# The last two blocks' gate, choice and ranking in another order, expert 0's gate weights by themselves, and one looped body for further tiles

## The chip, the core and the metric

The kernel runs on one core of a Trainium2 chip. The core has five engines that work side by side, each through its own instructions in order: TensorE (PE in the profile, with its weight loads as PEld), VectorE (DVE), ScalarE (ACT), GpSimd (POOL) and SyncE (SP, which here only starts DMA transfers). They wait for one another by semaphores. The metric is the device time of one execution in microseconds (us); less is better.

## What is computed

Attention over 4 x 576 tokens with 8 heads, a dense layer with g = h cos(h), and a mixture of 8 experts of which every token uses two. The part that matters here is the third:

```python
def _moe2_ref(x, w_gate, w_noise, noise, w1, w2):          # x: 2304 x 512
    noisy_logits = x @ w_gate + np.log1p(np.exp(x @ w_noise)) * noise
    top2 = np.argpartition(-noisy_logits, 2, axis=1)[:, :2]
    top2_w = softmax of the two chosen logits
    for e in range(8):                                     # w1: 512 x 1024, w2: 1024 x 512
        for k in range(2):
            mask = top2[:, k] == e
            h = np.maximum(x[mask] @ w1[e], 0.0)
            out[mask] += top2_w[mask, k, None] * (h @ w2[e])
```

All of it is float32. The kernel writes each float32 operand as a sum of two fp32r halves ("hi" and "lo") and runs three matmul passes (hi x hi, hi x lo, lo x hi) where float32 accuracy is wanted. Making the two halves is called a split: ACT copies the hi half, another engine subtracts it from the original to give the lo half.

## The kernel before

The 2304 tokens go through attention and the dense layer as 9 blocks of 256 tokens (blocks 0 to 8, `NBLK` = 9, `LAST` = 8). For each block there are 8 pairs p: `g1` gives the hidden values (PE, L562), `post` turns them into g (ACT and DVE, with a last subtraction on POOL, L570 to L579) and `g2` adds them into two output tiles in PSUM (PE `acc`, L589). The pairs are the steps 0 to 71 of one loop, with `g2` two steps behind `g1`; the table `BESIDE` says which other work is put beside which step and at which of four places in it (-1, 0, 1, 2). Scheduling is manual: on every engine the instructions run in the order in which the Python code issues them.

When a block's `acc` tiles are complete, its tokens are sent to the experts in a chain of small steps: `r_rows` (the block's rows x leave PSUM and go to DRAM `x1d`), `r_trans` (PE transposes, tiles `mx`, `x1t`), `r_gate` (PE, `mg`, `lp`), `r_logits` (PE `ml`, DVE `lg`, `az`), `r_exp` (ACT), `r_top`, `r_top2` (DVE, the softplus of the noise as a series, tile `po`), `r_pick` (DVE, the two best experts of each token, ending in the tile `os`), `r_rank` (PE counts the tokens ahead, tile `mr`; DVE makes slots `si` from it) and `r_send` (POOL, four indirect DMAs that write token number and logit difference into the table `tab`). For blocks 0 to 7 these steps lie beside later blocks' matmuls. For block 8 there is no later block; they lie beside the first half of expert 0.

An expert has room for 608 tokens in five tiles (128, 128, 96 and 128, 128). `m_g1(e, half, f)` makes hidden chunk f of 8 for the first 352 tokens (half 0, PE L903 `pe`, input `xga`) or for the other 256 (half 1, input `xgb`); ACT (L905) and DVE (L906) evacuate it as the halves of `h`, through two PSUM buffers `ph` (in half 0 of expert 0 every second f uses the buffers of `acc` instead). `m_y(e, t)` multiplies `h` with the second weight (PE L938 `ye`), `m_out` scales by the gate weight and sends the rows to `out`. Expert 0's first 352 tokens are final before the last two blocks are ranked, so its half 0 starts right after block 8's last `acc` matmul. Its tiles 3 and 4 can only be gathered when block 8's sends have landed: `t_load` reads `tab` back (SP, `tb`), `t_gather` fetches the rows (POOL, `xg`), `t_trans` transposes them (PE `mgx` L886) and splits them into `xgb` (ACT L888, DVE L889). `t_weights` makes all gate weights from `tb` (L852 to L861, with one exp on ACT).

Expert weights are loaded as `wraw` and split by `split_we(e, k, q)` into `we` (ACT L819; L820 on DVE, or on POOL where the call says so); expert 0 has 16 such pieces of 128 x 512.

At the end, DVE reduces the token counts `cnt` (L1094 to L1100), every engine loads one number (L1101), and a branch (L1102) jumps over code for tokens beyond an expert's 608. With these inputs that code is not executed. It stands there eight times, once for each expert, each with a loop of its own.

Of the kernel before, what the change touches and what calls it, by code (L numbers as in the profile page):

```python
# [9 lines left out]
F32 = mybir.dt.float32  # L10
# [8 lines left out]
P = 128  # L19
# [7 lines left out]
DM = 512  # L27
# [172 lines left out]
70:2 r_pick(7)  # L200
71:2 r_rank(7)
# [6 lines left out]
def kernel(ctx: ExitStack, tc: tile.TileContext, qT, kT, v, wm, we, wg, noise, out):  # L208
# [408 lines left out]
    def r_gate(blk):  # L617
# [4 lines left out]
        lp = tpool.tile([P, TB], F32, tag="t4", name=f"lp{blk}")  # L622
# [160 lines left out]
    for blk in range(NBLK - 1):  # L783
# [11 lines left out]
        at_step(i0 + d[0] + d[1], 2, r_rank, blk)  # L795
# [49 lines left out]
    def t_weights():  # L845
        weight_of(wts, tb.rearrange("p e t c -> p (e t) c")[:, :, 1])

    def weight_of(dst, d):
# [116 lines left out]
    for q in range(4):  # L965
# [3 lines left out]
        if q < 2:  # L969
            at_step(69, 2, split_we, 0, 1, q)  # L970
# [40 lines left out]
    tasks = {}  # L1011
# [81 lines left out]
    mxc = small.tile([P, 1], F32, tag="mxc", name="mxc", bufs=1)  # L1093
    nc.vector.tensor_reduce(mxc, cnt, axis=AX.X, op=ALU.max)  # L1094
    nti = small.tile([P, NE + 1], I32, tag="nti", name="nti", bufs=1)
    ntf = small.tile([P, NE], F32, tag="ntf", name="ntf", bufs=1)
    nc.vector.tensor_scalar(ntf, cnt, float(CAP), None, op0=ALU.max)
    nc.vector.tensor_scalar(ntf, ntf, 1.0 / P, (63.5 - CAP) / P + NTILE, op0=ALU.mult, op1=ALU.add)
    nc.vector.tensor_copy(nti[:, :NE], ntf)
# [86 lines left out]
```

## Time and profile before

| | |
|---|---|
| time, median of 3 executions | 1034.81 us (1034.64 to 1035.19) |
| the profiled execution's own time | 1032.98 us |
| its span, first to last instruction | 1031.2 us |
| PE matmul busy | 980.9 us (95% of the span) |
| DVE, ACT, POOL busy | 547.5, 458.7, 368.1 us |
| chain of work that ended last, by engine | PE 72%, DVE 13%, ACT 5%, DMA 4% |

The profile lists every instruction with its start, its duration and, where its engine stood idle before it, who released it. The span is the time that instructions cover; the execution's own time is a little longer. Times in the text are us from the start of the span. [...]

### The profile page before, as it was taken

How to read it: one execution, taken by the hardware profiler on the slowest of the kernel's cores; microseconds unless marked ns; L12 is line 12 of the kernel's file. 1: busy time of each engine (PE TensorE's matmuls, PEld its weight loads, DVE VectorE, ACT ScalarE, POOL GpSimd, SP SyncE). 2: the span in 40 equal slices, each digit the busy share in tenths (PEclk: the TensorE clock that was granted, in tenths of full speed). 3: DMA queues.
4: the chain of work that ended last, by engine and by line, in shares of the span. 5: the costliest groups of instructions: out<-in, count | busy, mean ns of one | idle time of the engine just before them, and what ended most of it. 6: DMA issues, size and time to landing. Idle time of an engine off the chain costs nothing.

```text
span 1031.2 us, 16810 instructions
## 1 busy us (share of the span) xinstructions
PE 980.9 (95%) x6560; PEld 864.8 (84%) x6560; DVE 547.5 (53%) x1134; ACT 458.7 (44%) x908; POOL 368.1 (36%) x477
## 2 busy tenths in 40 slices
PE   8797989999999899999999889999999999999995
PEld 6676778988889788898887689898898979898984
DVE  7799885357754655354464556344453536353221
ACT  6646765555645655455554334233232414142110
POOL 5555553243453341323334432231313232322211
PEclk9998999999999999999999999999999999999998
DMA  9962212223312120000054345453434243441201
GB/s 216 328 220 81 80 55 43 85 72 114 96 52 57 40 55 1 21 1 23 21 192 122 84 134 176 140 168 110 156 126 157 76 154 124 157 149 55 67 26 47
DMA packets 70601, 105.19 MB, mean 102 GB/s; under 512 B 31251, under 2 KB 44819, under 8 KB 70512
## 3 DMA queue, kind: packets, MB, share of 16 engines
q1 hardware_dynamic: 60528, 76.34, 24.3%
q0 software_dynamic: 9984, 27.68, 8.7%
q8 instruction: 54, 0.88, 0.4%
q14 instruction: 35, 0.29, 0.1%
HBM read 85.41 MB, written 19.59 MB: 102 GB/s over the span
## 4 chain that ended last, share of the span: by engine, by line
PE 72%; DVE 13%; ACT 5%; DMA 4%; issue 3%; SPq 1%; POOL 1%; ACTq 0%; DVEq 0%; POOLq 0%
PE pe L903 20%; PE ye L938 20%; PE ph L562 13%; PE acc L589 12%; DVE cut L291 3%; DMA raw<-in_wm 2%; PE sc L430 2%; PE mgx L886 2%; DVE cut L290 1%; DVE cut L292 1%; DVE r L571 1%; PE mo L505 1%; DVE po L654 1%; PE mt L485 1%; DVE r L575 1%
## 5 line engine op out<-in xcount | busy, mean ns | idle before, releaser
L562 PE MATMUL ph<-xhl,wm 128*128 128x256 f32 x1728 | 230.0, 289 | 11.6 <-ACT wm L298 4.3
L562 PEld LDWEIGHTS ph<-xhl,wm 128*128 128x128 f32 x1728 | 219.4, 195 | 19.9 <-ACT wm L298 4.7
L938 PE MATMUL ye<-we,h 128*128 128x512 f32 (+1 forms) x960 | 231.0, 397 | 0.0
L589 PE MATMUL acc<-wm,g 128*128 128x512 f32 x864 | 220.3, 398 | 2.8 <-POOL wm L299 0.9
L938 PEld LDWEIGHTS ye<-we,h 128*128 128x128 f32 (+1 forms) x960 | 173.9, 184 | 43.3
L589 PEld LDWEIGHTS acc<-wm,g 128*128 128x128 f32 x864 | 156.8, 190 | 33.7 <-POOL wm L299 1.2
L579 POOL TENSOR_TENSOR g<-r,g 128x512 fp32r<-128x512 f32 x72 | 95.7, 1329 | 207.5 <-ACT g L578 207.4
L903 PE MATMUL pe<-xga,we 128*128 128x352 f32 x768 | 125.4, 323 | 0.0
L903 PEld LDWEIGHTS pe<-xga,we 128*128 128x128 f32 x768 | 122.7, 188 | 0.5 <-issue 0.4
L951 POOL DMA_INDIRECT out<-old,tir x35 | 35.6, 1017 | 221.9 <-DVE old L949 217.1
L906 DVE SCALAR_TENSOR_TENSOR h<-pe,h 128x256 fp32r<-128x256 f32 (+1 forms) x128 | 60.6, 474 | 97.1 <-ACT h L905 96.2
L905 ACT ACTIVATE h<-pe 128x256 fp32r<-128x256 f32 (+1 forms) x128 | 54.2, 424 | 122.2 <-PE pe L903 122.2
L949 DVE SCALAR_TENSOR_TENSOR old<-ye,wts,old 128x512 f32<-128x512 f32 (+1 forms) x35 | 26.3, 750 | 135.5 <-PE ye L938 135.5
L903 PE MATMUL pe<-xgb,we 128*128 128x256 f32 x768 | 95.9, 286 | 1.8 <-DVE xgb L889 1.3
L903 PEld LDWEIGHTS pe<-xgb,we 128*128 128x128 f32 x768 | 94.7, 195 | 2.5 <-DVE xgb L889 1.5
L571 DVE SCALAR_TENSOR_TENSOR r<-r,ph 128x512 f32<-128x512 int32 x72 | 49.1, 682 | 82.9 <-ACT r L570 82.8
L575 DVE SCALAR_TENSOR_TENSOR r<-r,ph 128x512 f32<-128x512 f32 x72 | 49.4, 686 | 82.2 <-ACT r L574 82.0
L820 DVE TENSOR_TENSOR we<-wraw,we 128x512 fp32r<-128x512 f32 x121 | 82.5, 691 | 3.6 <-ACT we L819 0.9
L819 ACT ACTIVATE we<-wraw 128x512 fp32r<-128x512 f32 x128 | 78.4, 623 | 3.2 <-issue 3.2
L573 ACT ACTIVATE r<-r 128x512 f32<-128x512 f32 x72 | 45.4, 631 | 65.5 <-DVE r L571 65.4
L570 ACT ACTIVATE r<-ph 128x512 int32<-128x512 f32 x72 | 42.6, 592 | 51.1 <-PE ph L562 50.9
L578 ACT ACTIVATE g<-r 128x512 fp32r<-128x512 f32 x72 | 45.4, 631 | 43.8 <-DVE r L575 29.5
(181 smaller groups left out, 1035.3 us busy)
## 6 DMA issues: line engine op xcount, KB each, us to landing
wraw<-in_we SPq DMA_DIRECT2D x64, 512.0 KB, 5.7
raw<-in_wm SPq DMA_DIRECT2D x28, 512.0 KB, 9.8
vts<-in_v SPq DMA_DIRECT2D x13, 384.0 KB, 3.9
x1d<-x SPq DMA_DIRECT2D x9, 512.0 KB, 3.6
out<-zt SPq DMA_DIRECT2D x18, 256.0 KB, 3.9
kts<-in_kT SPq DMA_DIRECT2D x13, 288.0 KB, 3.1
qts<-in_qT SPq DMA_DIRECT2D x26, 144.0 KB, 3.9
piece<-in_wm SPq DMA_DIRECT2D x4, 512.0 KB, 4.0
```

The lines of the kernel that those rows point to most:

```text
L562: nc.tensor.matmul(ph[:, j, :], w[:, a, o:o + P], t[:, x, c, :], start=(c == 0 and n == 0 and (j == 0 or len(cs) == 4)), stop=(c == 3 and ...
L571: nc.vector.scalar_tensor_tensor(r, n, -TWO_PI, ph, op0=ALU.mult, op1=ALU.add)
L573: nc.scalar.activation(r, r, AF.Sin, scale=0.5)
L575: nc.vector.scalar_tensor_tensor(r, r, 0.5, ph, op0=ALU.subtract, op1=ALU.mult)
L579: nc.gpsimd.tensor_tensor(g[:, 1, :], r, g[:, 0, :].bitcast(F32), op=ALU.subtract)
L589: nc.tensor.matmul(ACC[blk][t], g[:, a, j * TB + t * P:j * TB + (t + 1) * P], w[:, x, 1024 + j * DM:1024 + (j + 1) * DM], start=(p == 0 an ...
L819: nc.scalar.activation(t[:, 0, fs], raw, AF.Copy)
L820: eng.tensor_tensor(t[:, 1, fs], raw, t[:, 0, fs].bitcast(F32), op=ALU.subtract)
L903: nc.tensor.matmul(ph[:, :n], w[:, a, o:o + P], x[:, b, c, :], start=(c == 0 and i == 0), stop=(c == 3 and i == 2))
L905: nc.scalar.activation(h[:, 0, f, :], ph[:, :n], AF.Relu)
L906: nc.vector.scalar_tensor_tensor(h[:, 1, f, :], ph[:, :n], 0.0, h[:, 0, f, :].bitcast(F32), op0=ALU.max, op1=ALU.subtract)
L938: nc.tensor.matmul(acc, h[:, a, f, o:o + n], w[:, b, (f % 4) * DM:(f % 4 + 1) * DM], start=(f == 0 and i == 0), stop=(f == 7 and i == 2))
```

## The change

It has four parts.

1. In steps 70 and 71, `split_we(0,1,2)` and `split_we(0,1,3)` are done beside the last two pairs of block 8, and `r_pick(7)` moves from step 70 to the end of step 71, with `split_we(0,2,0)` behind it. `r_rank(7)` moves from step 71 to behind the last `g2` and `r_rows(8)`, and `r_send(7)` with it.
2. `r_rows(8)` moves its second half with DVE instead of ACT, ahead of it ACT executes one dummy exp, and block 8's steps are placed anew among expert 0's `m_g1`: the transposes ahead of chunk 0, the gate behind chunk 0, and so on, with the ranking between chunks 6 and 7. The splits of expert 0 that POOL did (its L820 in this stage) are done by DVE. `lp` of block 8 gets another buffer.
3. `t_weights` makes expert 0's five gate weights first (5 columns) and those of experts 1 to 7 (35 columns) behind `m_out(0, 0..2)`.
4. The code for further tokens stands once, in a loop over tiles with a loop over experts in it. It is still jumped over.

```diff
-70:2 r_pick(7)
-71:2 r_rank(7)
+70:1 split_we(0,1,2)
+71:0 split_we(0,1,3)
+71:2 r_pick(7) split_we(0,2,0)
...
     def r_rows(blk):
         for t in range(2):
-            nc.scalar.activation(x[:, t, :], ACC[blk][t], AF.Copy, scale=-2.0)
+            if blk == NBLK - 1 and t:
+                nc.vector.tensor_scalar(x[:, t, :], ACC[blk][t], -2.0, None, op0=ALU.mult)
+            else:
+                nc.scalar.activation(x[:, t, :], ACC[blk][t], AF.Copy, scale=-2.0)
...
     g2(*steps[-2])
-    for t in range(2):
-        r_send(NBLK - 2, t)
     g2(*steps[-1])
     LAST = NBLK - 1
+    nc.scalar.activation(one, one, AF.Exp)
     r_rows(LAST)
+    r_rank(LAST - 1)
+    for t in range(2):
+        r_send(LAST - 1, t)
...
-    for f, t in ((0, r_trans), (1, r_gate), (2, r_logits), (3, r_exp), (3, r_top), (4, r_top2), (5, r_pick), (7, r_rank)):
-        tasks.setdefault(f, []).append(t)
-    late = [(1, 2), (1, 3)] + [(2, q) for q in range(4)] + [(3, 0), (3, 1)]
-    for f in range(8):
-        m_g1(0, 0, f)
-        split_we(0, *late[f], nc.gpsimd if f < 7 else nc.vector)
-        for t in tasks.get(f, []):
-            t(LAST)
-    for q in range(2, 4):
+    r_trans(LAST)
+    m_g1(0, 0, 0)
+    r_gate(LAST)
+    m_g1(0, 0, 1)
+    split_we(0, 2, 1)
+    r_logits(LAST)
+    r_exp(LAST)
+    split_we(0, 2, 2)
+    r_top(LAST)
+    m_g1(0, 0, 2)
+    r_top2(LAST)
+    m_g1(0, 0, 3)
+    r_pick(LAST)
+    for f in range(4, 7):
+        m_g1(0, 0, f)
+    r_rank(LAST)
+    m_g1(0, 0, 7)
+    split_we(0, 2, 3)
+    for q in range(4):
         split_we(0, 3, q)
...
+    t_weights(0, 1)
     t_load(1, NE)
-    t_weights()
...
     for t in range(3):
         m_out(0, t)
+    t_weights(1, NE)
...
     with tc.If(over > CAP):
-        for e in range(NE):
-            nt = nc.values_load(nti[0:1, e:e + 1], min_val=NTILE, max_val=NTILE + -(-(NT - CAP) // P))
-            with tc.For_i(NTILE, nt, 1) as i:
+        nt = nc.values_load(nti[0:1, 1:2], min_val=NTILE, max_val=NTILE + -(-(NT - CAP) // P))
+        with tc.For_i(NTILE, nt, 1) as i:
+            with tc.For_i(0, NE, 1) as e:
```

The first place is DVE in the last two steps of block 8. `r_7` is the tile of the last pair; `oh`, `os` belong to the pick of block 7 and `rb`, `base` to its rank. Before:

```order
L681 CAST fi_5772<-i_5763 128x4
L684 TENSOR_TENSOR oh_5774<-iota_184,fi_5772 128x16 x2
L687 TENSOR_TENSOR os_5777<-oh_5774 128x16
L571 SCALAR_TENSOR_TENSOR r_7_5804<-r_7_5804,ph_7_5779 128x512
L575 SCALAR_TENSOR_TENSOR r_7_5804<-r_7_5804,ph_7_5779 128x512
L699 TENSOR_TENSOR rb_5831<-mr_5825,base 128x16
L701 TENSOR_TENSOR base<-mr_5825,base 128x8
```

And now (`we_1` are the two weight splits):

```order
L576 SCALAR_TENSOR_TENSOR r_6_5741<-r_6_5741,ph_6_5716 128x512
L828 TENSOR_TENSOR we_1_5708<-wraw_0_5497,we_1_5708 128x512
L572 SCALAR_TENSOR_TENSOR r_7_5789<-r_7_5789,ph_7_5764 128x512
L828 TENSOR_TENSOR we_1_5708<-wraw_0_5497,we_1_5708 128x512
L576 SCALAR_TENSOR_TENSOR r_7_5789<-r_7_5789,ph_7_5764 128x512
L680 MAX m_5812<-po_5692 128x8
L681 MAX_INDEX i_5813<-m_5812,po_5692 128x8
```

The pick of block 7 stood ahead of the last pair's two operations on DVE and now stands behind them; two splits stand among them.

The second place is PE behind block 8's last `acc`, among expert 0's chunks `pe_0_0` to `pe_0_7`. Before:

```order
L903 MATMUL pe_0_0_5885<-xga_5594,we_0_5555 128x352 x12
L613 MATMUL mx_0_5903<-ident,x_8_5872 128x128 x4
L613 MATMUL mx_1_5909<-ident,x_8_5872 128x128 x4
L903 MATMUL pe_0_1_5915<-xga_5594,we_0_5555 128x352 x12
L621 MATMUL mg_5932<-x1t_5902,wgn 32x256 x4
L903 MATMUL pe_0_2_5939<-xga_5594,we_0_5555 128x352 x12
L630 MATMUL ml_5957<-ident,lp_5937 128x128 x2
L903 MATMUL pe_0_3_5964<-xga_5594,we_0_5555 128x352 x12
L903 MATMUL pe_0_4_5997<-xga_5594,we_1_5708 128x352 x12
L903 MATMUL pe_0_5_6019<-xga_5594,we_1_5708 128x352 x12
L903 MATMUL pe_0_6_6053<-xga_5594,we_1_5708 128x352 x12
L903 MATMUL pe_0_7_6071<-xga_5594,we_1_5708 128x352 x12
```

And now:

```order
L617 MATMUL mx_0_5893<-ident,x_8_5857 128x128 x4
L617 MATMUL mx_1_5899<-ident,x_8_5857 128x128 x4
L912 MATMUL pe_0_0_5906<-xga_5594,we_0_5555 128x352 x12
L625 MATMUL mg_5921<-x1t_5892,wgn 32x256 x4
L912 MATMUL pe_0_1_5928<-xga_5594,we_0_5555 128x352 x12
L637 MATMUL ml_5945<-ident,lp_5926 128x128 x2
L912 MATMUL pe_0_2_5970<-xga_5594,we_0_5555 128x352 x12
L912 MATMUL pe_0_3_5990<-xga_5594,we_0_5555 128x352 x12
L912 MATMUL pe_0_4_6022<-xga_5594,we_1_5708 128x352 x12
L912 MATMUL pe_0_5_6037<-xga_5594,we_1_5708 128x352 x12
L912 MATMUL pe_0_6_6052<-xga_5594,we_1_5708 128x352 x12
L700 LDWEIGHTS tri
```

Block 8's transposes, gate and logits stand one chunk earlier, and its rank (`tri` is its first operand) stands ahead of the last chunk instead of behind it.

The third place is DVE where expert 0's second half begins. Before:

```order
L820 TENSOR_TENSOR we_1_6144<-wraw_0_6115,we_1_6144 128x512 x4
L852 SCALAR_TENSOR_TENSOR we__6169<-tb 128x40
L854 TENSOR_SCALAR wts<-we__6169 128x40
L855 RECIPROCAL wts<-wts 128x40
L856 TENSOR_SCALAR wn__6170<-tb 128x40
L858 TENSOR_SCALAR wo__6176<-we__6169 128x40
L859 TENSOR_TENSOR wn__6170<-wn__6170,wo__6176 128x40
L860 TENSOR_TENSOR wn__6170<-wn__6170,we__6169 128x40
L861 TENSOR_TENSOR wts<-wts,wn__6170 128x40
L889 TENSOR_TENSOR xgb_6250<-mgx_3_6251,xgb_6250 128x4x128
L889 TENSOR_TENSOR xgb_6250<-mgx_4_6258,xgb_6250 128x4x128
L946 TENSOR_SCALAR new_6275<-ye_0_6181,wts 128x512
```

And now:

```order
L870 TENSOR_TENSOR wts<-wts,wn__6155 128x5
L898 TENSOR_TENSOR xgb_6251<-mgx_3_6252,xgb_6251 128x4x128
L898 TENSOR_TENSOR xgb_6251<-mgx_4_6259,xgb_6251 128x4x128
L955 TENSOR_SCALAR new_6276<-ye_0_6182,wts 128x512
L955 TENSOR_SCALAR new_6282<-ye_1_6207,wts 128x512
L955 TENSOR_SCALAR new_6288<-ye_2_6232,wts 96x512
L861 SCALAR_TENSOR_TENSOR we__6294<-tb 128x35
L863 TENSOR_SCALAR wts<-we__6294 128x35
```

The eight operations on all 40 weights stood ahead of the splits of `xgb`; now eight on 5 columns stand there, and eight on 35 columns behind the three `new`, ahead of the first evacuation of half 1.

## Rows read from the trace of the kernel before

**Rows 1.** Busy time by stretch: stretch, its length, each engine's busy us, PEclk, DMA.

```profile
545.00:604.00 59.00, 49.78 (x266) 41.83 (x266) 30.74 (x88) 20.16 (x39) 28.50 (x39) 0.94 0.42 112
604.00:1019.00 415.00, 414.91 (x2433) 370.67 (x2431) 175.11 (x294) 123.44 (x256) 111.05 (x176) 1.00 0.37 122
1019.00:1031.20 12.20, 0.00 (x0) 0.00 (x0) 1.25 (x6) 0.00 (x0) 1.00 (x1) 0.61 0.09 28
```

**Rows 2.** PE's waits between 540 and 604: total us, times, longest.

```profile
PE mr L693 <- DVE os L687: 5.0, 2, 3.7
PE mgx L886 <- DMA xg<-x1d,tic: 1.4, 2, 1.1
PE pe L903 <- DVE xgb L889: 1.3, 1, 1.3
```

**Rows 3.** Two short stretches, columns as in rows 1.

```profile
574.50:577.90 3.40, 3.37 (x13) 2.70 (x14) 3.30 (x11) 0.42 (x1) 0.82 (x1) 0.50 0.00 0
...
598.40:601.80 3.40, 3.40 (x18) 3.40 (x17) 2.03 (x4) 0.38 (x1) 2.33 (x5) 0.50 0.54 176
```

**Rows 4.** PE in order of time: start, us, line, operation, count, idle before.

```profile
542.09 2.91 PE L589 MATMUL acc<-wm,g 128*128 128x512 f32 x12
...
551.08 2.56 PE L589 MATMUL acc<-wm,g 128*128 128x512 f32 x10 [0.68 <-POOL spacer L713]
...
561.01 9.78 PE L903 MATMUL pe<-xga,we 128*128 128x352 f32 x60
...
574.68 17.07 PE L938 MATMUL ye<-we,h 128*128 128x512 f32 x66
...
593.83 0.66 PE L886 MATMUL mgx<-ident,xg 128*128 128x128 f32 x4 [1.11 <-DMA xg<-x1d,tic]
...
598.09 5.95 PE L903 MATMUL pe<-xgb,we 128*128 128x256 f32 x35 [1.32 <-DVE xgb L889]
```

**Rows 5.** ACT in order of time, columns as in rows 4.

```profile
544.39 0.58 ACT L570 ACTIVATE r<-ph 128x512 int32<-128x512 f32 x1
...
564.20 1.28 ACT L640 ACT_TABLE_LOAD   x1
```

**Rows 6.** DVE in order of time, columns as in rows 4.

```profile
537.53 1.44 DVE L654 SCALAR_TENSOR_TENSOR po<-po,s 128x16 f32<-128x16 f32 x7
...
546.15 0.68 DVE L571 SCALAR_TENSOR_TENSOR r<-r,ph 128x512 f32<-128x512 int32 x1
...
566.87 4.42 DVE L654 SCALAR_TENSOR_TENSOR po<-po,s 128x16 f32<-128x16 f32 x7
...
594.89 0.20 DVE L852 SCALAR_TENSOR_TENSOR we__6169<-tb 128x40 f32<-128x40 f32 x1 [11.94 <-DMA tb<-tab]
...
597.95 2.05 DVE L946 TENSOR_SCALAR new<-ye,wts 128x512 f32<-128x512 f32 x3
```

**Rows 7.** POOL in order of time, columns as in rows 4.

```profile
566.66 2.71 POOL L820 TENSOR_TENSOR we<-wraw,we 128x512 fp32r<-128x512 f32 x2 [1.12 <-ACT we L819]
```

**Rows 8.** One DVE group from 558 to 575: count, busy us, mean ns, idle before.

```profile
L906 DVE SCALAR_TENSOR_TENSOR h<-pe,h 128x352 fp32r<-128x352 f32 x7 | 3.5, 518 | 2.4 <-ACT h L905 2.4
```

**Rows 9.** The page's group of DVE's splits, columns as in rows 8.

```profile
L820 DVE TENSOR_TENSOR we<-wraw,we 128x512 fp32r<-128x512 f32 x121 | 82.5, 691 | 3.6 <-ACT we L819 0.9
```

**Rows 10.** Line L1102: engine, count, ns min/median/max, first and last start.

```profile
L1102 PEldq COMPARE_BRANCH  x1: 4012/4012/4012, 1020.9 to 1020.9; - x1
L1102 SPq COMPARE_BRANCH  x1: 45/45/45, 1021.2 to 1021.2; - x1
L1102 POOLq INC_SWDGE_SEM  x1: 1015/1015/1015, 1025.9 to 1025.9; - x1
```

**Rows 11.** POOL's last DMA issue in order of time, columns as in rows 4.

```profile
1019.98 1.00 POOL L951 DMA_INDIRECT out<-old,tir  x1 [4.35 <-DVE ntf L1097]
```

**Rows 12.** SP's waits from 1015 on, columns as in rows 2.

```profile
SPq L1102 <- SPq L1102: 3.8, 1, 3.8
```

**Rows 13.** Output DMAs of experts 1 to 7: count, median us from issue to landing.

```profile
out<-old,tir POOLq DMA_INDIRECT x35, 2.8
```

More of the change, by code (lines that the diff above doesn't have):

```diff
@@ L621, in r_gate @@
             nc.tensor.matmul(mid[32 * c:32 * c + 32, :TB], wgn[:, c, :], xt[:, c, :], start=True, stop=True)
-        lp = tpool.tile([P, TB], F32, tag="t4", name=f"lp{blk}")
+        if blk < NBLK - 1:
+            lp = tpool.tile([P, TB], F32, tag="t4", name=f"lp{blk}")
+        else:
+            lp = c1.tile([P, DM], F32, tag="old", name=f"lp{blk}", bufs=3)[:, :TB]
         nc.vector.tensor_copy(lp, mid[:, :TB])
@@ L856, in weight_of @@
         nc.vector.tensor_scalar(nm, d, 0.0, None, op0=ALU.is_le)
-        one = c2.tile([P, NE * NTILE], F32, tag="wo_", name="wo_", bufs=1)[:, :n]
-        nc.vector.tensor_scalar(one, e_, -1.0, 1.0, op0=ALU.mult, op1=ALU.add)
-        nc.vector.tensor_tensor(nm, nm, one, op=ALU.mult)
+        lin = c2.tile([P, NE * NTILE], F32, tag="wo_", name="wo_", bufs=1)[:, :n]
+        nc.vector.tensor_scalar(lin, e_, -1.0, 1.0, op0=ALU.mult, op1=ALU.add)
+        nc.vector.tensor_tensor(nm, nm, lin, op=ALU.mult)
         nc.vector.tensor_tensor(nm, nm, e_, op=ALU.add)
@@ L1090 @@
                 load_we(e + 2, 0, t - 1)
[L1093 to L1099, printed above, removed]
@@ L1100 @@
-    nc.vector.tensor_copy(nti[:, NE:], mxc)
-    over = nc.values_load(nti[0:1, NE:NE + 1], min_val=0, max_val=NT)
+    mxc = small.tile([P, 2], F32, tag="mxc", name="mxc", bufs=1)
+    nc.vector.tensor_reduce(mxc[:, 0:1], cnt, axis=AX.X, op=ALU.max)
+    nti = small.tile([P, 2], I32, tag="nti", name="nti", bufs=1)
+    nc.vector.tensor_scalar(mxc[:, 1:2], mxc[:, 0:1], float(CAP), None, op0=ALU.max)
+    nc.vector.tensor_scalar(mxc[:, 1:2], mxc[:, 1:2], 1.0 / P, (63.5 - CAP) / P + NTILE, op0=ALU.mult, op1=ALU.add)
@@ L1113 @@
                 weight_of(w, gtb[:, 1:2])
-                x = tpool.tile([P, DM], F32, tag="t4", name=f"gx{e}")
+                x = tpool.tile([P, DM], F32, tag="t4", name="gx")
                 nc.gpsimd.indirect_dma_start(out=x, out_offset=None, in_=x1d,
                                              in_offset=bass.IndirectOffsetOnAxis(ap=idc[:, :1], axis=0))
-                od = c1.tile([P, DM], F32, tag="old", name=f"go{e}", bufs=3)
+                od = c1.tile([P, DM], F32, tag="old", name="go", bufs=3)
@@ L1118 @@
                 nc.gpsimd.indirect_dma_start(out=od, out_offset=None, in_=out,
                                              in_offset=bass.IndirectOffsetOnAxis(ap=idc[:, :1], axis=0))
-                wt = [ring.tile([P, 2, 2048], F32, tag="ring", name=f"gw{e}_{j}") for j in range(2)]
+                wt = [ring.tile([P, 2, 2048], F32, tag="ring", name=f"gw_{j}") for j in range(2)]
                 for j in range(2):
-                    nc.sync.dma_start(wt[j], we[2 * e + j])
-                mid = psum.tile([P, 512], F32, tag="mid", name=f"gm{e}", bufs=2)
+                    nc.sync.dma_start(wt[j], we[bass.ds(2 * e + j, 1)].rearrange("o p k f -> p (o k) f"))
@@ L1124 @@
+                mid = psum.tile([P, 512], F32, tag="mid", name="gm", bufs=2)
                 for c in range(4):
                     nc.tensor.transpose(mid[:, c * P:(c + 1) * P], x[:, c * P:(c + 1) * P], ident)
-                xt = c2.tile([P, 4, P], F32, tag="xgb", name=f"gxt{e}")
+                xt = c2.tile([P, 4, P], F32, tag="xgb", name="gxt")
                 nc.vector.tensor_copy(xt, mid.rearrange("p (c q) -> p c q", q=P))
-                h = c2.tile([P, 8, P], F32, tag="h1", name=f"gh{e}")
+                h = c2.tile([P, 8, P], F32, tag="h1", name="gh")
@@ L1129 @@
                 for f in range(8):
-                    ph = psum.tile([P, 512], F32, tag="ph", name=f"gp{e}_{f}", bufs=2)
+                    ph = psum.tile([P, 512], F32, tag="ph", name=f"gp_{f}", bufs=2)
                     for c in range(4):
@@ L1135 @@
                     nc.scalar.activation(h[:, f, :], ph[:, :P], AF.Relu)
-                acc = psum.tile([P, DM], F32, tag="acc", name=f"gy{e}", bufs=4)
+                acc = psum.tile([P, DM], F32, tag="acc", name="gy", bufs=4)
                 for f in range(8):
```

23 lines of the change are left out of this document (13 added, 10 removed).

## The prediction

> **What bounds the kernel now.** I began with busy time by stretch. From 604 to 1019 us PE is busy 414.91 of 415.00 us: experts 1 to 7 are PE's alone, and whatever comes earlier in front of 604 comes earlier at the end. From 545 to 604, the hand-over from block 8 to expert 0, PE is busy 49.78 of 59.00 us, so it is idle for 9.2 us. From 1019 on no matmul runs, and still 12.2 us pass [rows 1]. All that the change moves lies in these two stretches. PE's waits say what the 9.2 us are made of: 5.0 us for `os`, the end of a pick (once for block 7, and 3.7 us for block 8), 1.4 us for the gathered rows, 1.3 us for the lo half of `xgb` [rows 2]. Two more losses are no idle time. For 3.4 us each, from 574.5 and from 598.4, the granted clock was 0.50, both times behind a gap of PE (3.7 us; then two gaps within 3 us, the second 1.3) [rows 2 to 4]. At half speed each costs 1.7 us. So the stretch has some 12.6 us to give.
>
> **Last pair of block 8.** PE is through with step 69's `acc` at 545.00 (542.09 + 2.91) [rows 4]. ACT has the last pair's first result at 544.97 (544.39 + 0.58) [rows 5], yet DVE takes it up at 546.15, because the pick of block 7 stands in front [rows 6]. In the new order the pick is behind, so DVE starts at 545.0: 1.15 us earlier. The chain from there (sine, square, DVE, ACT, POOL) is as long as it was, so the last ten `acc` matmuls move from 551.08 to 549.9 and end at 552.5 instead of 553.64 [rows 4]. The two splits added there lie in DVE's waits for ACT (sine and square); if one is late it costs at most its own 0.69 us [rows 9]. The dummy exp brings a table load of 1.28 us [rows 5] onto ACT. ACT's last half for the pair is ready one POOL subtraction (half of 2.71 us [rows 7]) ahead of those ten matmuls, at 548.5; with a split's copy and the load ACT is free at 550.5, and the first `acc` tile is complete at 551: covered by about 0.5 us, and the load is gone from block 8's exp. The pick costs PE nothing now, since the rank stands behind `acc`.
>
> **Choice of block 8.** PE: rank 0.15, then the transposes, whose second half waits for DVE's copy of `acc` (a third of 2.05 us, so 0.68 [rows 6]) and takes 0.45: 553.6. Seven chunks by 9.78 / 5 = 1.96 us [rows 4] and 0.85 for gate and logits: PE stands before the rank of block 8 at 568.2. DVE: the logits are there at 558.5 (553.6, two chunks, 0.85). In front of them DVE has chunk 1's evacuation behind ACT's, and a split: 560.0. Then come 30 small operations; seven of them took 1.44 us in block 7, 0.206 each, but 4.42 in block 8 [rows 6]. In that second case POOL was subtracting splits from 566.66 to 569.37 [rows 7]; DVE then seems to wait with operations that have two operands in SBUF. The change takes POOL's splits out of this stage, so I use 0.206: 6.2 us. With two evacuations (0.52 each [rows 8]), one split (0.69 [rows 9]) and about 0.9 for the exp and the split's copy on ACT the pick ends at 568.8. Its last 13 operations partly don't depend on each other, so this is an upper end; the lower one is PE's 568.2. I take 568.5, so the rank is done at 568.65 instead of 574.68 [rows 4]: 6.0 us earlier, and the wait of 3.7 us is gone.
>
> **To the end of half 0.** One chunk now follows the rank: 570.6. The 66 `ye` matmuls took 17.07 us [rows 4] with 3.4 us at clock 0.50 [rows 3]; without that 15.4 us: 586.0. The splits of the second weight, four of which now come behind the last evacuation on DVE, must be there from 572.5 on, one each 0.7 us; DVE has the first at 572 and gives one each 0.69 us [rows 9]. That is covered by about 0.5 us only; without cover it costs that lateness, once. Ranks, sends, table loads and gathers are not changed: from the end of the rank to the second gathered tile on PE it took 593.83 - 574.68 = 19.15 us [rows 4], which gives 587.8. So PE waits 1.3 us there, as it did.
>
> **Second half of expert 0.** Before, the lo half of `xgb` stood behind all gate weights, which themselves waited for all 16 table loads (594.89 [rows 6]); that was the 1.3 us. Now only five weights stand in front, made long before. Transposes 0.45, six `ye` 1.4: PE begins `pe` half 1 at 589.65. A chunk of 12 is estimated from the 352-column rows as 1.96 x 256 / 352 = 1.43 us, so two are done at 592.5. The third needs the first one's PSUM buffer, and here the change adds a wait: DVE has the `new` tiles (2.05) and then the 35 weights in front of that evacuation. The weights took 597.95 - 594.89 less two splits, 1.9 us [rows 6], and ACT's evacuation stands behind their exp. DVE: 591.5, 593.4, evacuated 593.85. PE waits 1.35 us and ends the third chunk at 595.3. Before, the same three chunks ended at 598.09 + 5.95 = 604.04 [rows 4]. The hand-over gains 8.7 us. The waits left, 1.3 and 1.35 us with 4.7 us of work between, are about as long as one that was followed by clock 1.00 (5.0 - 3.7 = 1.3 us, of the first wait for `os` [rows 2]), so I count no half clock. If all splits and picks come late by what they may (0.7 + 0.5 + 0.6) the gain is 6.9; if the two waits shrink to nothing it is up to 10.5.
>
> **The end.** PE's branch over the unused code took 4.01 us, to 1025, and POOL's closing of its queue starts at 1025.9 [rows 10]. The last output is issued at 1019.98 [rows 11]. The jump was some 770 instructions on PE (half weight loads) and 107 to 161 on the others, and is 104 and 24 to 28 with one body. No row shows a jump that short. Bounds: nothing is saved, because SP too stood still for 3.8 us after its branch [rows 12], with a jump of only 113; or all 4.0. In between is the landing of the last output: with the 2.8 us that this queue takes [rows 13] it is there at 1022.8, and POOL's closing can start at 1022.9 or 1023.0 rather than 1025.9. I take 2.9 us, since the one jump that shows a long branch becomes the seventh part of itself. [...]
>
> **Sum.** 8.7 + 2.9 = 11.6 us off the span of 1031.2, so 1019.6. The profiled execution's own time (1032.98) is 1.8 us above its span and 1.83 us under the median (1034.81); I take both as they are: 1034.81 - 11.6 = **1023.2 us**.
>
> **Rivals.**
> *A short jump stalls too.* For it: SP's 3.8 us. Against: on SP the branch itself is short, only PE's row has a long one. Then 1034.81 - 8.7 = 1026.1.
> *The clock falls once more, or DVE is late in the hand-over.* For it: DVE now has seven splits more and two waits over 1 us stay. One fall to 0.50 costs 1.7 us, late splits and pick 1.8: 1025.0.
> *VectorE becomes the bound.* The seven `po` operations lasted 2.98 us longer in block 8, as if three of them had waited 1.0 us each. If that came from DVE's fuller queue and not from POOL, it can hit all 19 of the 30 operations that have two operands in SBUF, 1.0 us each, all of it on PE's wait for the rank: 1023.2 + 19 = 1042; slower than before from the twelfth on (11.6 us). Against it: the same seven took 0.206 each with POOL idle [rows 6].
> *The change does nothing at the end* is the first rival; that the order is as written is plain from the engines' rows.
>
> **How the numbers follow.** Forecast 0.52 (1021.8 to 1024.3), short jump 0.21, clock or late DVE 0.22, DVE as the bound 0.03, and 0.02 for something faster. The range reaches from the full 4.0 us at the end with a slightly better hand-over (1021.0) to the first rival with a further 1.3 us lost (1027.4). 0.2%, 2.1 us, is what a measurement of this kernel can tell from no change; only the third rival comes near: faster 0.96, same 0.02, slower 0.02.
>
> **What the changed kernel's profile would show.** The last ten `acc` matmuls at about 550; no table load in block 8's exp; the seven `po` operations in about 1.5 us; PE waiting under 1 us for the rank of block 8, which ends near 568.7; the second gathered tile near 588; no wait for `xgb`, but 1.0 to 1.6 us before the third chunk of half 1; clock 1.00 from 545 on; half 1's third chunk done near 595; PE without a gap from there; and a branch on PE of under 0.1 us with about 8 us from the last DVE operation on `old` to the end. A po group still near 4 us, a clock of 0.50, or a branch of 4 us again would make it wrong.

## The result, and the profile after

The changed kernel took 1022.11 us (median of 4 runs, 1020.52 to 1022.43), the kernel before 1034.72 us (4 runs, 1032.17 to 1035.19): the ratio is 0.9878, with a 95% interval of 0.9858 to 0.9898, or 12.6 us less. The forecast was 1023.2 us, in a range of 1021.0 to 1027.4. In the profiled execution the span fell by 12.4 us, from 1031.2 to 1018.8.

The stretches of the hand-over and of the experts, as in [rows 1] (stretch, length, busy us of PE, its weight load, DVE, ACT, POOL, granted clock, DMA share, GB/s):

```profile
545.00:595.50 50.50, 47.53 (x270) 39.68 (x269) 34.10 (x114) 20.23 (x41) 19.10 (x32) 1.00 0.49 124
595.50:1007.00 411.50, 411.11 (x2416) 367.78 (x2415) 174.67 (x292) 123.18 (x256) 110.73 (x176) 1.00 0.38 123
```

PE was idle for 9.2 us of the hand-over; now for 3.0, and the granted clock (PEclk, TensorE's clock as a share of its full speed) is 1.00 instead of 0.94. Its waits from 540 to 600 us (total, times, longest) answer to [rows 2]. The waits for `os` and for `xgb` are gone, and one before a chunk of half 1 is new:

```profile
PE pe L912 <- DVE h L915: 1.1, 1, 1.1
PE acc L590 <- POOL spacer L720: 0.7, 1, 0.7
PE acc L590 <- POOL g L580: 0.5, 1, 0.5
PE mgx L895 <- DMA xg<-x1d,tic: 0.5, 1, 0.5
```

PE, then DVE, in order of time, as in [rows 4, 6]:

```profile
550.74 2.58 PE L590 MATMUL acc<-wm,g 128*128 128x512 f32 x10 [0.69 <-POOL spacer L720]
...
569.03 0.18 PE L700 MATMUL mr<-os,tri 128*128 128x8 bf16 x1
...
571.18 15.52 PE L947 MATMUL ye<-we,h 128*128 128x512 f32 x66
...
587.60 0.66 PE L895 MATMUL mgx<-ident,xg 128*128 128x128 f32 x4 [0.46 <-DMA xg<-x1d,tic]
...
593.82 1.70 PE L912 MATMUL pe<-xgb,we 128*128 128x256 f32 x12 [1.14 <-DVE h L915]
```

```profile
545.80 0.69 DVE L572 SCALAR_TENSOR_TENSOR r<-r,ph 128x512 f32<-128x512 int32 x1 [0.64 <-ACT r L571]
...
564.31 1.44 DVE L661 SCALAR_TENSOR_TENSOR po<-po,s 128x16 f32<-128x16 f32 x7
```

The rank of block 8 starts without a wait, the 66 `ye` matmuls take 15.52 us instead of 17.07, and the seven `po` operations 1.44 instead of 4.42. The end (on line L1123 the branch over the unused code and POOL's first semaphores behind it, then the closing of POOL's queue, POOL's drain, and SP's wait for the last output) answers to [rows 10, 12]:

```profile
L1123 POOLq EVENT_SEMAPHORE  x2: 17/30/42, 1013.3 to 1013.4; - x2
...
L1123 POOLq COMPARE_BRANCH  x1: 54/54/54, 1013.1 to 1013.1; - x1
L1123 PEldq COMPARE_BRANCH  x1: 228/228/228, 1013.1 to 1013.1; - x1
...
L1123 POOLq INC_SWDGE_SEM  x1: 1017/1017/1017, 1013.5 to 1013.5; - x1
...
L1203 POOLq DRAIN  x3: 46/107/3422, 1014.6 to 1018.5; - x3
...
SPq L1203 <- DMA out<-old,tir: 0.8, 1, 0.8
```

**Where the 12.4 us came from.** I cut each profile at three points: A, the start of the last 24 `ph` matmuls (step 71); the end of the third chunk of half 1 of expert 0; and the start of the last DVE operation on `old`. That gives the lead A, the hand-over H, the experts E and the end T. The table has all kernels of this study; each number is the difference of two rows of its profile.

| kernel | A | H | E | T | time, us |
|---|---|---|---|---|---|
| before | 539.22 | 64.82 | 414.91 | 12.25 | 1034.72 |
| after | 540.02 | 55.50 | 415.60 | 7.68 | 1022.11 |
| after, again | 541.47 | 55.91 | 414.94 | 7.68 | 1020.63 |
| e1, loop only | 542.24 | 65.04 | 414.94 | 7.68 | 1030.73 |
| e2, eight loops | 542.99 | 55.45 | 415.58 | 12.38 | 1027.73 |
| e3, short PE | 540.43 | 63.35 | 415.25 | 12.37 | 1034.32 |
| e9, long PE | 540.39 | 64.92 | 414.99 | 7.70 | 1030.27 |
| e10, long POOL | 542.16 | 64.93 | 414.95 | 8.16 | 1031.66 |
| e11, longer POOL | 541.81 | 65.06 | 414.95 | 11.08 | 1034.62 |
| e6, part 1 | 541.63 | 62.52 | 414.92 | 12.33 | 1033.94 |
| e12, splits on DVE | 540.29 | 62.31 | 414.90 | 12.60 | 1032.50 |
| e4, splits on POOL | 543.06 | 56.32 | 415.49 | 7.73 | 1024.26 |
| e5, weights whole | 543.51 | 56.45 | 414.94 | 7.70 | 1024.20 |
| e8, weights late | 541.25 | 54.30 | 414.95 | 7.70 | 1020.22 |

So the hand-over gave 9.3 us and the end 4.6; the lead took 0.8 back and the experts 0.7. A varies from 539.2 to 542.2 us among the kernels with the old order and from 540.0 to 543.5 among those with the new one, though within each group the code there is the same (but for the edit of e6 in step 70), so an effect under 2 us is read from H, E or T rather than from the total. The median of before was 1034.72 us with the first result, then 1035.21 (beside e1, e2, e3, e9), 1035.63 (e4, e5, e6, e10) and 1034.46 (e8, e11, e12, after again).

### The profile page after: what moved, and what is told of

It is laid out like the page before. It is cut to its first block, busy times and chain, and to the rows that moved or that the text cites. A ratio compares the mean times of both kernels' runs of the same rounds, so it can differ in the third digit from the quotient of the medians.

```text
span 1018.8 us, 16807 instructions
## 1 busy us (share of the span) xinstructions
PE 979.7 (96%) x6560; PEld 864.1 (85%) x6560; DVE 551.1 (54%) x1149; ACT 458.2 (45%) x909; POOL 358.4 (35%) x470
## 4 chain that ended last, share of the span: by engine, by line
PE 69%; DVE 13%; ACT 6%; DMA 5%; issue 4%; POOL 1%; SPq 1%; ACTq 0%; POOLq 0%; DVEq 0%
PE ye L947 20%; PE pe L912 20%; PE ph L563 12%; PE acc L590 11%; DVE cut L292 3%; DMA raw<-in_wm 2%; PE mgx L895 2%; DVE r L572 1%; DVE cut L291 1%; PE sc L431 1%; DVE cut L293 1%; DVE r L576 1%; ACT r L574 1%; ACT r L575 1%; PE mo L506 1%
## 5 line engine op out<-in xcount | busy, mean ns | idle before, releaser
L828 DVE TENSOR_TENSOR we<-wraw,we 128x512 fp32r<-128x512 f32 x128 | 88.9, 704 | 4.2 <-ACT g L579 0.9
```

The lines of the kernel that those rows point to most:

```text
L828: eng.tensor_tensor(t[:, 1, fs], raw, t[:, 0, fs].bitcast(F32), op=ALU.subtract)
```

## Experiments on the end

**e1: the looped body alone, on the kernel before.**

```diff
-        for e in range(NE):
-            nt = nc.values_load(nti[0:1, e:e + 1], ...)
-            with tc.For_i(NTILE, nt, 1) as i:
+        nt = nc.values_load(nti[0:1, 1:2], ...)
+        with tc.For_i(NTILE, nt, 1) as i:
+            with tc.For_i(0, NE, 1) as e:
```

> The kernel before with the looped body alone; the two hand-overs stay as they were. Theory (what the end lost was the jump over eight bodies and the code that each engine then had to fetch): PE's closing branch takes 0.2 us instead of 4.0, the end of the kernel from the last operation on `old` falls from 12.25 to about 7.7 us, and the time from 1034.7 to about 1030.1 us. Rival (the closing of POOL's queue waits for the landing of the last output, as the prediction had it): 2.9 us less, 1031.8 us. Second rival (the end is shorter in the changed kernel for something that came before it, such as fewer transfers still open): no gain, 1034.7 us.

1030.73 us against 1035.21 (ratio 0.9961, 0.9947 to 0.9975); T is 7.68 instead of 12.25. (The edit takes the reduction of the counts on DVE along. It moves nothing: the branch starts 2.0 us behind the last operation on `old`, as before.) The 4.6 us belong to this part alone, and both rivals fall (2.9 us for the landing, nothing for something ahead of the end).

**e2: the changed kernel with the eight bodies.** The edit is that of e1 the other way round.

> The changed kernel with its eight written-out bodies put back; everything ahead of the end as in the changed kernel. Theory (the parts add up): the end is 12.2 us again, PE's branch 4.0, and the time 1022.1 + 4.6 = 1026.7 us; the hand-over from block 8 to expert 0 is as in the changed kernel, PE idle for some 3 us from 545 to 595. Rival (the looped body changes the engines' code ahead of it too, and with it the fetches in the hand-over): the hand-over is longer as well, by a us or more, and the time is 1028 us or above.

1027.73 us (ratio 0.9924, 0.9908 to 0.9941): T is 12.38 again and H, 55.45, is that of the changed kernel (55.50). The parts add up.

**e3: eight bodies, but hardly any matmul in them.**

```diff
-                    for c in range(4):
-                        nc.tensor.matmul(ph[:, :P], ...)
...
-                for f in range(8):
-                    nc.tensor.matmul(acc, h[:, f, :], ...)
+                nc.tensor.matmul(acc, h[:, 7, :], ...)
```

> The kernel before, with its eight bodies, but PE's part of each cut to three matmuls (one transpose, one of the first and one of the second product; left out are the other 41, in code that no token of these inputs reaches). PE's jump is so about a sixth of what it was; those of ACT, DVE, POOL and SP stay at 107 to 161 instructions. Theory (the stall belongs to PE's jump, the only one with a long branch in the rows): PE's branch under 0.3 us, the end about 7.7 us, 1030.1 us. Rival (each engine pays for its own jump, SP's 3.8 us being one): the others still stop for some 3 to 4 us, the end stays at 11 to 12 us, 1034 us.

The theory fell. PE's branch is short, and nothing is gained: 1034.32 us (ratio 0.9992, 0.9981 to 1.0002), T 12.37. The rows of the branch's line (engine, operation, count, ns min/median/max, first and last start) show that the other engines stop all the same:

```profile
L1102 SPq EVENT_SEMAPHORE  x9: 17/17/17, 1025.2 to 1025.8; - x9
L1102 POOLq EVENT_SEMAPHORE  x5: 17/43/43, 1025.6 to 1026.0; - x5
...
L1102 POOLq COMPARE_BRANCH  x1: 58/58/58, 1021.0 to 1021.0; - x1
L1102 PEldq COMPARE_BRANCH  x1: 445/445/445, 1021.0 to 1021.0; - x1
...
L1102 SPq COMPARE_BRANCH  x1: 45/45/45, 1021.3 to 1021.3; - x1
```

On SP and POOL the branch itself is over at once, and the stop shows only as the gap up to the first semaphore behind it: from 1021.3 to 1025.2 on SP and from 1021.1 to 1025.6 on POOL. POOL's rows of the kernel before show the same stop, from 1021.0 to 1025.5:

```profile
L1102 POOLq EVENT_SEMAPHORE  x5: 17/43/43, 1025.5 to 1025.8; - x5
...
L1102 POOLq COMPARE_BRANCH  x1: 58/58/58, 1020.9 to 1020.9; - x1
```

In the changed kernel the gap is some 0.2 us (1013.1 to 1013.3, above).

**e9: the loop, with PE's matmuls in it eight times over.**

```diff
-                    for c in range(4):
+                    for n, c in enumerate(8 * [0, 1, 2, 3]):
...
-                for f in range(8):
+                for n in range(64):
```

> The kernel before with the looped body, but with PE's matmuls in it written out eight times over (code that no token of these inputs reaches, so the output is the same): PE's jump is as long as it was, those of the other four engines are 24 to 28 instructions. Theory (a long jump of PE is enough): PE's branch 4.0 us, the end 11 to 12.2 us, 1034 us. Rival (the 4 us come about because five engines fetch at once and wait for each other's transfers): PE alone is served in under 2.5 us, the end is 10 us or less, 1032.5 us or less.

PE's branch takes 3.97 us, as much as in the kernel before (4.01), where five engines stop, so on PE's stop the theory held and the rival fell; but 1030.27 us (ratio 0.9955, 0.9938 to 0.9972) and T 7.70 say that this stop costs nothing. The same line, and POOL's drain:

```profile
L1100 POOLq EVENT_SEMAPHORE  x2: 17/30/43, 1022.5 to 1022.6; - x2
...
L1100 PEldq EVENT_SEMAPHORE  x2: 51/51/51, 1026.4 to 1026.5; - x2
...
L1100 PEldq COMPARE_BRANCH  x1: 3972/3972/3972, 1022.3 to 1022.3; - x1
...
L1181 POOLq DRAIN  x3: 46/107/3422, 1023.8 to 1027.7; - x3
```

PE goes on at 1026.4, and POOL's drain, begun at 1023.8, lasts until 1027.2 anyway. The 4.0 us lie under it.

**e10 and e11: the loop, with 130 or 300 small memsets on POOL in it.**

```diff
+                for _ in range(130):      # e11: range(300)
+                    nc.gpsimd.memset(spacer, 0.0)
```

> The kernel before with the looped body, and in it 130 small memsets more on POOL (in code that no token of these inputs reaches): POOL's jump is over 100 instructions as it was, those of PE, ACT, DVE and SP are short. The runs so far: PE's branch of 4 us alone costs nothing (end 7.8 us), the others' jumps alone cost all of it. New theory (POOL's own jump is the one on the path: its queue's closing of 1.0 us and its drain of 3.4 stand behind it): the end is 11.5 to 12.5 us again, 1034.7 us. Rival (SP's stop of 3.8 us is the one, since SP makes the last waits): the end stays near 7.7 us, 1030.4 us.

1031.66 us (ratio 0.9967, 0.9955 to 0.9979), T 8.16: POOL did not stop, so e10 by itself decided nothing between POOL and SP. It made me count lengths again, this time in machine instructions of the built programs; a line of the listing is often several of them.

> The kernel before with the looped body and 300 small memsets more on POOL in it (code that no token of these inputs reaches). With 130, POOL's jump of some 173 machine instructions did not stop it. Counted in the built programs (a line of the listing is often several machine instructions), the jumps of the kernel before were about 360 on SP, 302 on POOL, 286 on ACT, 319 on DVE; here POOL's is about 343 and the other three stay at 36 to 45. New theory (a jump beyond a length between 173 and 286 stops these engines, and POOL's stop is the one on the path): POOL stands still for 3.5 to 4.5 us after its branch, the end from the last operation on `old` is 11.5 to 12.3 us, 1034.7 us. Rival (the stop comes of the eight written-out loops with their branches, not of the length): the end is 7.7 to 8.2 us, 1030.5 us. Second rival (SP's stop makes the end): likewise 7.7 to 8.2 us, but with POOL's stop in the trace.

POOL's rows in e10, then in e11:

```profile
L1100 POOLq EVENT_SEMAPHORE  x3: 17/17/43, 1024.6 to 1024.8; - x3
...
L1100 POOLq COMPARE_BRANCH  x1: 54/54/54, 1024.1 to 1024.1; - x1
```

```profile
L1100 POOLq EVENT_SEMAPHORE  x3: 17/17/43, 1027.3 to 1027.5; - x3
...
L1100 POOLq COMPARE_BRANCH  x1: 58/58/58, 1023.8 to 1023.8; - x1
...
L1100 POOLq INC_SWDGE_SEM  x1: 1029/1029/1029, 1027.6 to 1027.6; - x1
```

With a jump of 343 instructions POOL stands from 1023.9 to 1027.3, and the closing and the drain follow: T 11.08, 1034.62 us against 1034.46 (ratio 0.9999, 0.9989 to 1.0010). POOL's stop alone brings back 3.4 of the 4.6 us; the other four engines, whose jumps are short here, do not stop. T says this, not the total, in which a long lead (541.81) hides that the end is shorter than before. The trace bears it out in every kernel with its end read here (before, after, e1, e2, e3, e9, e10, e11): from the start of POOL's closing to the end of the kernel it is 5.3 us (1025.9 to 1031.2 before, 1013.5 to 1018.8 after, 1027.6 to 1032.9 here), whichever engines stop. T stays 1.2 us under that of before, and under the 11.5 to 12.3 us expected, because POOL's stop is 3.4 us alone and 4.5 with the others. Why it is longer when five engines stop was not tried, nor was a stop of SP alone.

## Experiments on the hand-over

**e6: part 1 alone, on the kernel before.**

```diff
-70:2 r_pick(7)
-71:2 r_rank(7)
+70:1 split_we(0,1,2)
+71:0 split_we(0,1,3)
+71:2 r_pick(7) split_we(0,2,0)
...
     g2(*steps[-1])
...
+    r_rank(LAST - 1)
+    for t in range(2):
+        r_send(LAST - 1, t)
```

> The kernel before with its first part alone: the pick of block 7 behind the last pair's first pass on DVE, its rank and sends behind the last `acc`, the splits (0,1,2), (0,1,3), (0,2,0) made on DVE in the last steps; the seven splits left are on POOL during the choice of block 8, as before. Theory: DVE takes up the last pair's result 1.1 us earlier, the choice of block 8 begins 1.1 us earlier and everything behind it comes along: 1033.6 us. Rival (the choice of block 8 ends when POOL's splits let it, not by its start): what is gained in the last pair is waited off before the rank of block 8, 1034.7 us.

The total can't tell (1033.94 against 1035.63 us, ratio 0.9990, 0.9974 to 1.0006); the trace can. PE's first wait and the rank of block 8:

```profile
PE mr L694 <- DVE os L688: 3.7, 1, 3.7
```

```profile
576.01 0.19 PE L694 MATMUL mr<-os,tri 128*128 128x8 bf16 x1 [3.73 <-DVE os L688]
```

And the same matmul in the kernel before:

```profile
574.53 0.19 PE L693 MATMUL mr<-os,tri 128*128 128x8 bf16 x1 [3.73 <-DVE os L687]
```

From A to the start of that rank it is 34.38 us, against 35.31 before: 0.93 us less, with the same wait of 3.7. (The last ten `acc` start 1.13 us earlier; the rank of block 7, which now stands behind them, takes most of the rest.) The whole choice moved along, and the rival falls. (H fell by 2.3 us. What is more than 0.93 lies in half 1, in 35 matmuls that took 4.45 us and 5.95 before, see the last section.)

**e12: the kernel before with the seven splits of that stage on DVE.**

```diff
-        split_we(0, *late[f], nc.gpsimd if f < 7 else nc.vector)
+        split_we(0, *late[f], nc.vector)
```

> The kernel before with the seven splits among the choice of block 8 on DVE instead of POOL, all else in its old order. Theory (each subtraction on POOL stops DVE's small operations until it ends): the seven `po` operations take 1.4 us instead of 4.4 and the `az` operation 0.2 instead of 1.0, that is 3.8 us; DVE has 4.8 us of splits more, most of them in its waits for PE and ACT ahead of the exp; PE's wait of 3.7 us for the rank of block 8 falls to 1.5 us or less, and the time is 1031 to 1033 us. Rival (the order makes the choice late, and DVE merely trades POOL's stops for work of its own): the wait stays at 3 us or more, 1034.7 us.

1032.50 us against 1034.46 (ratio 0.9985, 0.9975 to 0.9994). The seven `po` operations, and PE's waits:

```profile
568.28 1.44 DVE L654 SCALAR_TENSOR_TENSOR po<-po,s 128x16 f32<-128x16 f32 x7
```

```profile
PE mr L693 <- DVE os L687: 3.2, 2, 2.0
PE mgx L886 <- DMA xg<-x1d,tic: 3.0, 2, 2.2
```

DVE's stops vanish with POOL's subtractions, in the old order too. But the wait for the rank falls only from 3.7 to 2.0 us, between the two expectations, because DVE now carries those splits, three of 0.7 us between the logits and `os`. The rank starts 33.87 us after A (574.16), 1.44 us earlier than before; the waits for the gathered rows grow from 1.4 to 3.0 us. The changed kernel does both, it takes the splits off POOL and moves five of the seven out of the choice.

**e4: the changed kernel with two splits on POOL again.**

```diff
-    split_we(0, 2, 1)
+    split_we(0, 2, 1, nc.gpsimd)
...
-    split_we(0, 2, 2)
+    split_we(0, 2, 2, nc.gpsimd)
```

> The changed kernel with the two splits that lie among the choice of block 8, (0,2,1) and (0,2,2), on POOL again instead of DVE; nothing else moved. Theory (DVE's small operations with two operands in SBUF wait while POOL subtracts): two subtractions of 1.3 to 2.7 us cover part of the 30 operations, three or so of them take about 1.2 us instead of 0.2, the pick ends 2 to 3 us later although DVE has two splits of 0.69 us less, PE waits for the rank of block 8 for 1 to 2 us, and the time is 1023 to 1024.5 us. Rival (the choice is shorter because it stands in another order among the chunks, and POOL is innocent): the pick ends as early or up to 1.4 us earlier, PE does not wait, 1022.1 us.

POOL's two subtractions, and the two DVE operations that ran into them, in order of time:

```profile
563.57 1.29 POOL L828 TENSOR_TENSOR we<-wraw,we 128x512 fp32r<-128x512 f32 x1 [0.47 <-issue]
565.73 1.29 POOL L828 TENSOR_TENSOR we<-wraw,we 128x512 fp32r<-128x512 f32 x1 [0.88 <-ACT we L827]
```

```profile
563.88 1.00 DVE L642 SCALAR_TENSOR_TENSOR az<-lg 128x16 f32<-128x16 f32 x1
...
565.87 1.18 DVE L657 TENSOR_TENSOR s<-az 128x16 f32<-128x16 f32 x1
```

Both operations take 0.17 to 0.18 us in the changed kernel. Here each ends when POOL's ends (564.88 and 564.86; 567.05 and 567.02). So the mechanism is there, but my price was wrong: the stops cost 1.8 us, the splits that DVE no longer makes give 1.4 back, and the rank comes 29.03 us after A, as in the changed kernel (29.01), without a wait. So in the new order these two splits cost PE no more on POOL than on DVE. H is 0.4 to 0.8 us longer, all of it ahead of the second gathered tile; two profiles of the changed kernel differ there by 0.4. The time, 1024.26 us against 1035.63 (ratio 0.9898, 0.9871 to 0.9925), lies in the range expected by its long lead (543.06) only.

**e5: all gate weights at once, in their old place.**

```diff
-    t_weights(0, 1)
     t_load(1, NE)
+    t_weights(0, NE)
...
-    t_weights(1, NE)
```

> The changed kernel with all 40 columns of gate weights made at once, behind all table loads, where they were. Theory: the weights stand ahead of the lo half of `xgb` on DVE and wait for the last table load (issued at 587.0, so there at about 589), so that PE waits some 2 us before half 1, while the 1.1 us before its third chunk go: 0.9 us longer, 1023.0 us; with a half-clock stretch behind two waits close together, as in the kernel before, 2.6 us longer, 1024.7 us. Rival (the order of the weights is worth nothing, one wait only takes the place of the other): 1022.1 us.

PE's waits:

```profile
PE pe L912 <- DVE xgb L898: 1.3, 1, 1.3
...
PE pe L912 <- ACT xgb L897: 0.5, 1, 0.5
```

1.8 us of waits took the place of 1.1. From the second gathered tile (591.28) to the end of the third chunk it is 8.68 us, against 7.92 and 7.93 in the two profiles of the changed kernel: 0.75 us for this part. (H, with the scatter ahead of that tile, is 56.45 against 55.50 and 55.91.) The 66 `ye` took 15.52 us, as in the changed kernel, whose clock was 1.00 (17.07 before, with 3.4 us at 0.50), and the 35 matmuls behind the waits 4.46 (5.95 before). The rows of the two places in e5:

```profile
591.28 0.66 PE L895 MATMUL mgx<-ident,xg 128*128 128x128 f32 x4 [0.67 <-DMA xg<-x1d,tic]
...
595.50 4.46 PE L912 MATMUL pe<-xgb,we 128*128 128x256 f32 x35 [1.32 <-DVE xgb L898]
```

The time was 1024.20 us against 1035.63 (ratio 0.9891, 0.9863 to 0.9918).

**e8: the other 35 weights behind half 1; and the changed kernel again beside it.**

```diff
-    t_weights(1, NE)
...
     t_gather(1, 4)
+    t_weights(1, NE)
     for t in (3, 4):
```

> The changed kernel with the 35 gate weights of experts 1 to 7 made after the eight chunks of half 1 of expert 0 instead of ahead of them (their first use is in expert 1). Theory: DVE evacuates the first chunk of half 1 right after the `new` tiles, PE's wait of 1.1 us before the third chunk goes, and the time is 1.1 us under the changed kernel's of the same call. Rival (the 1.9 us of weights on DVE make PE wait at the place they go to): no gain, the same time.

> The changed kernel once more, on the chip on which the others of this call run, for comparison: 1022.1 us, or its ratio of 0.9878 to the kernel before. If the stretch ahead of step 71, whose code the change does not touch, lasts 540 to 543.5 us from run to run, the total scatters by as much, and the parts are to be compared by their own stretches; if it is the same within 0.3 us each time, by the totals.

The first three chunks of half 1 in e8, then the third one in the repeated run of the changed kernel:

```profile
590.91 4.64 PE L912 MATMUL pe<-xgb,we 128*128 128x256 f32 x36
```

```profile
595.68 1.70 PE L912 MATMUL pe<-xgb,we 128*128 128x256 f32 x12 [1.14 <-DVE h L915]
```

The wait of 1.14 us is gone and did not come back elsewhere: H is 54.30 instead of 55.50 and 55.91, and E is 414.95. In the totals it is 1020.22 against 1020.63 us (ranges 1019.91 to 1021.76 and 1020.26 to 1021.74), so the gain of 1.1 us is shown in the trace and not in the times. The ratios to before are 0.9866 (0.9850 to 0.9883) and 0.9864 (0.9847 to 0.9880).

## Why the prediction was right, and where it was not

**What PE waited for.** The waits that it names for the 9.2 us add up to 7.7. The rest are three short ones in the last pair and before half 1 (0.7, 0.5 and 0.3 us), of which the change removes little.

**Last pair, 1.15 us.** Right: in the changed kernel the last ten `acc` start 10.72 us after A, against 11.86 before, and in e6 10.73. The rank of block 8 comes 0.93 us earlier by it (e6).

**Choice of block 8, 6.0 us with the last pair.** Right in size: the rank starts 6.30 us earlier in relation to A (29.01 against 35.31). That POOL's subtractions stop DVE's small operations, as it assumed, is shown by e4 and e12; the 0.206 us for each of the seven was measured (1.44 in all). One thing was missed: the `az` operation had been stopped too, as this row of the kernel before shows.

```profile
562.46 1.00 DVE L635 SCALAR_TENSOR_TENSOR az<-lg 128x16 f32<-128x16 f32 x1
```

The prediction names operations with two operands in SBUF. In the kernel before one with a single operand was stopped as well: the cast below took 1.10 us instead of 0.17 and ended at 359.10, POOL's subtraction `g` at 359.07. The copy `lp`, which reads PSUM, was not: it took 0.42 us inside a subtraction of POOL from 559.46 to 560.75, and 0.41 in the changed kernel.

```profile
357.99 1.10 DVE L707 CAST si<-sf 128x4 int32<-128x4 f32 x1
...
560.03 0.42 DVE L623 COPY lp<-mg 128x256 f32<-128x256 f32 x1 [0.61 <-DMA x1d<-x]
```

```profile
357.78 1.29 POOL L579 TENSOR_TENSOR g<-r,g 128x512 fp32r<-128x512 f32 x1 [1.64 <-ACT g L578]
...
559.46 1.29 POOL L820 TENSOR_TENSOR we<-wraw,we 128x512 fp32r<-128x512 f32 x1 [1.44 <-ACT we L819]
```

What the 6.30 us are made of is shown in part only. e6 gives 0.93 for the last pair, e12 1.44 for the splits off POOL in the old order, where about half of PE's wait of 3.7 us stayed. The other 3.9 us come with the rest of the new order, in which block 8's steps stand a chunk earlier, five splits lie outside the choice and the exp's table load comes ahead of it. No run has the new order with all seven splits on POOL, so these are not told apart further.

**To the end of half 0, and half 1.** The second gathered tile came 47.58 us after A (47.98 the second time); forecast was 587.8 - 539.22 = 48.6. The new wait before the third chunk was 1.14 us, forecast 1.35, and the granted clock was 1.00. Hand-over: forecast 8.7, measured 9.3 and 8.9. (The 10.5 us given for both waits gone don't add up: 8.7 + 1.3 + 1.35 is 11.35. The range does not use it.)

**The end, 2.9 us forecast, 4.6 measured.** This step failed, in its reason and in its bounds of 0 to 4.0, though it pointed the right way.
- It took PE's branch of 4.0 us for the loss, since PE has the only long branch. e3 and e9 show that PE's stop is free under POOL's drain of 3.4 us. The loss was POOL's own stop of 4.5 us, shown by e11 and the constant 5.3 us behind it. No row of a branch shows it: on POOL it is a gap between the branch and the next semaphore.
- It let POOL's closing wait for the landing of the last output. The closing starts at 1013.5, 1.35 us after that output is issued (1012.15 in the chain of work below), less than the 2.8 us of [rows 13]. SP waits for the landing (0.8 us), beside the drain.

```profile
1012.15 1.00 POOL out L960
```

- It counted jumps in lines of the listing (113 on SP, 107 to 161 on the four engines). In machine instructions they were 286 to 360, and 36 to 45 with one body. SP's row therefore never was a jump short enough to speak for the first rival. That rival is refuted by e1: with one body no engine stops for more than about 0.5 us. PE's branch, for which the sign was under 0.1 us, took 0.23.

Of long jumps the runs show this: on POOL one of 173 machine instructions did not stop (e10) and one of 343 did, for 3.4 us (e11); on PE one of about 310 did not (0.45 us, e3) and one of about 1372 did (3.97 us, e9). Where between these lengths the stop begins was not tried. The profile also counts transfers of instructions, on two queues. In the kernel before, from 1008 us to the end (transfers, MB, share):

```profile
q8 instruction: 3, 0.05, 1.0%
q14 instruction: 8, 0.07, 0.8%
```

From 1008 us to the end (20 to 25 us) e3, where PE's jump is short and the others are long, has 2 on q8 and 8 on q14; e9, where PE's alone is long, 3 and 2; e11, where POOL's alone is, 1 and 4. That a stop is the wait for such transfers is my reading; no run shows it by itself.

**Rivals.** VectorE did not become the bound. The granted clock did not fall (1.00 in the hand-over), and DVE was not late. In the profile 12.4 us were gained where 11.6 were forecast: 1.7 more at the end and 0.6 more in the hand-over, less the 1.5 that the lead and the experts took. The median came out 1.1 us under the forecast. That it came so near is in part luck: the end gave 1.7 us more than forecast for a reason that was not seen, and the lead and the experts, of which the prediction counted nothing, took 1.5 back.

## What to carry to other kernels

At the end of a program look at each engine's first instruction behind the last branch, not only at the long branch: here POOL's closing decided, 5.3 us ahead of the end in all eight kernels read, and the jump over unused code stopped POOL when it was long (not with 173 machine instructions, but with 343). Subtractions on POOL beside a chain of small DVE operations stopped some of them (1.00 and 1.18 us instead of 0.17 and 0.18 in e4); move the work out of the chain's time rather than only to the other engine. A table that is made for all experts at once makes the first expert wait for it (0.75 us in e5).

## What was not expected

The lead, 540 us of the same code, varies by 3.0 us among the eight profiles with the old order and by 3.5 among the six with the new one. Of the change only the whole hand-over and the end are worth more. In a kernel as long as this, an edit of 1 us shows in its stretch and not in the total.

The granted clock after the same two waits of PE (0.49 and 1.32 us) before half 1, with the code of the kernel before, was not always the same. Here are the 35 matmuls behind them, in e3 and in e10. In e3, where they took 4.46 us, the clock was 1.00 from 598 to 604. In e10 they took 5.96, as in the kernel before (5.95), whose clock was 0.50 from 598.4 to 601.8 [rows 3]:

```profile
599.32 4.46 PE L903 MATMUL pe<-xgb,we 128*128 128x256 f32 x35 [1.32 <-DVE xgb L889]
```

```profile
601.13 5.96 PE L903 MATMUL pe<-xgb,we 128*128 128x256 f32 x35 [1.32 <-DVE xgb L889]
```

That is 1.5 us of H which comes and goes, and the reason why e3 and e6 have a shorter H. The runs differ ahead of it too. In e6 the 66 `ye` behind the wait for the rank took 18.11 us, and 17.07 in the kernel before; the waits for the gathered rows were 0.5 and 0.7 us in all in e3 and e6, instead of 1.4. What decides the clock stays open. So does the 0.6 us of E in the first profile of the changed kernel (415.60; 414.94 the second time; e2 and e4 have it too, 415.58 and 415.49). In the first profile 0.39 us of it is a wait of PE that the trace puts down to issue; ahead of it ACT took up the third chunk at 596.88, 1.36 us after its end, and the second time at once.
